# Batch 0's loads, its scores and the written order in a memory-attention and spatial-gate kernel

## The chip, the cores and the metric

One core of one Trainium2 chip runs the program. The metric is the device time of one execution in microseconds (us), lower is better. The engines are named as in the profile: PE (matrix products; PEld is its weight load), DVE (vector engine), ACT (scalar engine), POOL (GpSimd) and SP, which here only issues DMAs.

## The reference

```python
# attention through 32 memory slots; batch 8, 8 heads, 576 positions, head size 64
a   = softmax(phi, over positions)                 # phi: 8 x 8 x 576 x 32
k_m = einsum('bhsm,bhsd->bhmd', a, k)
v_m = einsum('bhsm,bhsd->bhmd', a, v)
attn = softmax(q @ k_m.T / 8)                      # over the 32 slots
x = (attn @ v_m), heads side by side               # 8 x 576 x 512
# gated unit
h = relu(x @ w_in)                                 # 512 -> 1024
u, v = h[..., :512], h[..., 512:]
v_n = (v - mean(v)) / sqrt(var(v) + 1e-6)
v_s = einsum('ts,bsd->btd', w_spatial, v_n) + b_spatial[None, :, None]
out = (u * v_s) @ w_out                            # 512 -> 512
```

w_in and w_out arrive as 64-bit floats, all other inputs as 32-bit floats.

## The kernel before

Eight batches go through the same chain of steps, and up to four batches are under way at a time. Each step is a Python generator with a letter, and each token of a written order advances one generator by one stage. A digit picks a tile (of 128 positions, of 128 channels, or a half of w_in), and each apostrophe means one batch further on. The letters are:

- P (`memory_weights`): phi is loaded, its maximum over positions is taken (DVE, then a transpose on PE `mt`, DVE `cm`, ACT `cmb`, a transpose back on PE `mb`), subtracted on DVE (L334), exponentiated on ACT (L342), and the sum `es` is taken.
- K (`memories`, for batch 0 `first_memories`): k and v are loaded into `kv_sb`, 144 small products with phi make `kvm`, `den` divides, `kmn` and `tk` turn k's part around.
- Q (`queries`, for batch 0 `first_queries`): q is loaded. For batch 0 PE transposes it (`tq`, L530), in later batches DVE does.
- S (`scores`, for batch 0 `first_scores`): q times the 32 memories (`sc`, L559 and L574), softmax on DVE and ACT, and the transposed weights `at`, split in a high part `ah` and a low part `al`.
- M (`products`): the 32 memories of v times one half of w_in, 512 columns wide (`mp`, L727), split into `mh` and `ml`. M1 makes the half for v, M0 the half for u.
- V (`gate`): `pv` (L760), relu, normalisation. U (`units`): `pu` (L844). G (`spatial`): `ps` (L880), fourteen pairs of products for each channel tile. O (`project`): `po` (L917) and the store.

Weights are prepared once, in steps of the same kind: D loads w_in in raw 64-bit words, E and L decode its v half and its u half (ACT, then POOL or ACT, then DVE L198), W loads w_spatial, T0 to T4 transpose it on PE (`wt`, `wr`, L260) and split it, B prepares the bias, X loads and decodes w_out. Z (`warm_up`) is a product of the constant `minus`, 128x128 by 128x512, whose result nothing reads; the order before has none of it.

The order around the change is written by hand: START for the first batches, then PLAN once for each of the batches 2 to 5, then END. Tokens become instructions in this order, and every engine works through its own instructions strictly in it. So an instruction that waits holds up whatever the order has behind it on the same engine. All loads and stores are issued by SP, which waits where a buffer is not yet free. The list `ON_VECTOR` names small operations that go to DVE in place of ACT or POOL. PSUM has eight banks, and every tile that PE writes, one of Z too, takes one of them in turn.

In batch 0 before, q is loaded as 1 KB runs (512 positions as four rows for each partition, then the last 64 positions), and SP issues in the order phi, q, k, rest of q, then weights, with v behind the first weights (L356). Scores of batch 0 are 64 products over 64 rows with 128 weight columns and 32 moving columns (L559), and 16 with 64 weight columns (L574).

## Time and profile before

| what | value |
|---|---|
| time, median of 3 runs | 421.88 us (417.91 to 422.09) |
| the profiled execution, its own time | 420.08 us |
| its span from first to last instruction | 418.3 us |
| PE busy | 395.1 us, 94% |
| DVE busy | 278.7 us, 67% |
| ACT busy | 223.7 us, 53% |
| POOL busy | 91.6 us, 22% |

The times of single instructions come from the one profiled execution. PE's busy time counts each product until its result has left the engine, while the next has begun, so a PE that is busy all the time need not be at its peak; what a product costs in a row of its kind is read from the chain, by the time of the row over its count. The profile also names the clock that PE was granted, as a share of the full 2.4 GHz.

### The profile page before, as it was taken

What the parts mean: (1) busy time and instruction counts of PE and PEld (TensorE: products, weight loads), DVE (VectorE), ACT (ScalarE), POOL (GpSimd) and SP (SyncE); (2) the same over time, 40 slices, a digit from 0 to 9 for tenths busy, and PEclk for the clock granted to TensorE, in tenths of its full rate; (3) what the DMA queues carried; (4) which work ended last, traced back from release to release, by engine and by line L of the source; (5) the groups of instructions that cost most, each with busy time, mean ns of one, the idle gap of its engine ahead of it and who ended that gap; (6) DMA issues with size and microseconds to landing.
All of it is one profiled execution on the core that took longest, in us unless ns stands there. A gap on an engine that the chain in (4) does not pass through costs nothing.

```text
span 418.3 us, 9443 instructions
## 1 busy us (share of the span) xinstructions
PE 395.1 (94%) x3906; PEld 342.8 (82%) x3906; DVE 278.7 (67%) x542; ACT 223.7 (53%) x457; POOL 91.6 (22%) x182
## 2 busy tenths in 40 slices
PE   0997999899999999999899999999999999999996
PEld 0784788688789897989699898989798888988984
DVE  2548989877987648955789258855787349854140
ACT  1436886336862378435853467435853485277122
POOL 1246475002300224013401034013401112032000
PEclk9998999999999999999999999999999999999999
DMA  8996968695572060927085712927400710000203
GB/s 254 328 382 219 199 97 279 121 226 159 84 198 55 25 215 18 258 95 130 2 211 131 132 53 56 228 92 132 53 2 0 133 51 2 0 2 26 76 0 125
DMA packets 86830, 50.69 MB, mean 121 GB/s; under 512 B 66754, under 2 KB 71874, under 8 KB 86788
## 3 DMA queue, kind: packets, MB, share of 16 engines
q1 hardware_dynamic: 86788, 50.10, 48.3%
q8 instruction: 30, 0.49, 0.5%
q14 instruction: 12, 0.10, 0.1%
HBM read 40.65 MB, written 9.44 MB: 120 GB/s over the span
## 4 chain that ended last, share of the span: by engine, by line
PE 80%; DMA 9%; DVE 5%; POOL 3%; issue 2%; ACT 1%; SPq 1%; POOLq 0%; DVEq 0%; ACTq 0%
PE ps L880 22%; PE po L917 22%; PE pu L844 12%; PE pv L760 10%; DMA phi_sb<-in_phi_dram 4%; PE mp L727 3%; PE kvm L434 3%; DMA kv_sb<-in_v_dram 2%; DMA q_all<-in_q_dram 2%; PE sc L559 2%; PE sc L661 1%; DVE phi_sb L334 1%; PE pv L776 1%; PE pv L768 1%; POOL half L289 1%
## 5 line engine op out<-in xcount | busy, mean ns | idle before, releaser
L880 PE MATMUL ps<-wth,vh 128*128 128x288 f32 x256 | 57.5, 304 | 1.1 <-DVE ml L163 0.6
L880 PE MATMUL ps<-wth,vl 128*128 128x288 f32 x256 | 54.7, 295 | 0.9 <-DVE vl L822 0.9
L880 PE MATMUL ps<-wtl,vh 128*128 128x288 f32 x256 | 54.6, 294 | 0.0
L805 DVE BATCH_NORM_STATS2 st<-vr 128x6 f32<-128x512 f32 (+1 forms) x40 | 27.3, 681 | 35.6 <-ACT vr L802 35.3
L917 PE MATMUL po<-woh,gh 128*128 128x512 f32 x128 | 50.4, 394 | 0.0
L917 PE MATMUL po<-woh,gl 128*128 128x512 f32 x128 | 50.0, 390 | 0.0
L917 PE MATMUL po<-wol,gh 128*128 128x512 f32 x128 | 49.9, 390 | 0.0
L923 ACT COPY o<-po 128x512 f32<-128x512 f32 x36 | 21.2, 588 | 53.2 <-PE po L917 35.7
L880 PEld LDWEIGHTS ps<-wth,vh 128*128 128x128 f32 x256 | 41.1, 188 | 5.8 <-issue 1.7
L880 PEld LDWEIGHTS ps<-wth,vl 128*128 128x128 f32 x256 | 40.9, 188 | 1.1 <-DVE vl L822 1.1
L880 PEld LDWEIGHTS ps<-wtl,vh 128*128 128x128 f32 x256 | 41.3, 188 | 0.0
L808 POOL TENSOR_SCALAR few<-few 128x1 f32<-128x1 f32 (+1 forms) x40 | 10.9, 272 | 132.2 <-DVE few L806 118.6
L844 PE MATMUL pu<-ah,mh 128*128 128x288 f32 x128 | 38.7, 302 | 0.0
L822 DVE TENSOR_TENSOR vl<-vr,vh 128x512 fp32r<-128x512 f32 x32 | 23.6, 741 | 21.7 <-ACT vh L820 21.7
L844 PE MATMUL pu<-al,mh 128*128 128x288 f32 x128 | 37.7, 295 | 0.0
L844 PE MATMUL pu<-ah,ml 128*128 128x288 f32 x128 | 37.6, 294 | 0.0
L893 DVE TENSOR_TENSOR g<-u,ps 128x288 f32<-128x288 f32 x64 | 26.5, 443 | 15.4 <-PE ps L880 14.8
L817 ACT ACTIVATE vr<-vr,few 128x512 f32<-128x512 f32 (+1 forms) x40 | 32.0, 816 | 5.2 <-POOL few L812 5.2
L899 ACT CAST gh<-g 128x512 fp32r<-128x512 f32 x32 | 19.7, 619 | 24.5 <-DVE g L893 24.4
L853 ACT ACTIVATE u<-pu 128x288 f32<-128x288 f32 x64 | 25.8, 418 | 5.7 <-PE pu L844 4.1
L917 PEld LDWEIGHTS po<-woh,gl 128*128 128x128 f32 x128 | 24.0, 188 | 5.2 <-DVE gl L901 0.2
L917 PEld LDWEIGHTS po<-woh,gh 128*128 128x128 f32 x128 | 24.0, 188 | 4.7
(174 smaller groups left out, 889.0 us busy)
## 6 DMA issues: line engine op xcount, KB each, us to landing
kv_sb<-in_k_dram SPq DMA_DIRECT2D x8, 1152.0 KB, 8.8
kv_sb<-in_v_dram SPq DMA_DIRECT2D x8, 1152.0 KB, 7.4
out_dram<-o SPq DMA_DIRECT2D x32, 256.0 KB, 2.4
q_sb<-in_q_dram SPq DMA_DIRECT2D x28, 288.0 KB, 8.7
phi_sb<-in_phi_dram SPq DMA_DIRECT2D x7, 576.0 KB, 4.2
raw<-in_moe_w_in_dram SPq DMA_DIRECT2D x4, 512.0 KB, 11.4
raw<-in_moe_w_in_dram SPq DMA_DIRECT2D x2, 1024.0 KB, 10.7
raw_out<-in_moe_w_out_dram SPq DMA_DIRECT2D x4, 512.0 KB, 5.1
```

The costliest lines, as they stand in the source:

```text
L434: nc.tensor.matmul(kvm[r][32 * j : 32 * j + 32], phi_sb[halves[r], j, i, :], kv_sb[halves[r], j, :, i * D : (i + 1) * D], start=(i == 0), ...
L760: nc.tensor.matmul(pv, x[:, r, cs], m[:, r, DM:DFF], start=(n == 0), stop=(n == 5))
L805: nc.vector.bn_stats(st6, vr)
L817: nc.scalar.activation(vr, vr, AF.Identity, bias=sh, scale=rs)
L822: nc.vector.tensor_tensor(vl[:, st, :], vr, vh[:, st, :].bitcast(F32), op=ALU.subtract)
L844: nc.tensor.matmul(pu[hf], m[:, r, cs], a[:, r, at[hf]], start=(r == 0 and n == 0), stop=(r == 1 and n == 2),)
L853: nc.scalar.activation(u[:, dt, at[hf]], pu[hf], AF.Relu)
L880: nc.tensor.matmul(ps[hf], a, w[:, hf * HALF : (hf + 1) * HALF], start=(n == 0), stop=(n == len(ops) - 1),)
L893: nc.vector.tensor_tensor(g[:, at], u[:, dt, at], ps[hf], op=ALU.mult)
L899: nc.scalar.copy(hi, x)
L917: nc.tensor.matmul(po, a, w, start=(n == 0), stop=(n == 11))
L923: nc.scalar.copy(o, po)
```

## The change

Six things are changed together.

- q of batch 0 is loaded in the layout of k and v, one run of nine positions (2,304 bytes) for each partition and pair of heads, and SP's order becomes phi, k, q, v.
- A helper `hold` lets POOL copy one landed element of a given load into the first words of a buffer that another load will fill. That load can then only be issued when the given load has landed and POOL has come to the copy. `HOLD` names the pairs: the two v-half loads of w_in wait for q and for v, the two u-half loads for the first and the third piece of the v half, w_spatial for the fourth.
- Scores of batch 0 become 40 products: two of a partition's nine positions are stacked on 128 rows, the memories `kd` stand on a diagonal of two blocks with zeros beside it (POOL clears it), with 64 weight columns and 64 moving columns (32 for the ninth position). Transposes, softmax and `at` follow the new layout, in three pieces of 16, 16 and 4 groups.
- The sum `es` of batch 0 is taken by four halving steps on DVE in place of one reduction. `kmn1` and `kd1` are added to `ON_VECTOR`.
- START is one order for all eight batches, in which `>` moves the base one batch on. PLAN and END are gone, and with them the loop.
- The order has 56 Z steps. 51 of them stand ahead of the products of M1, of these 10 ahead of `mt`, 3 between `mt` and `mb`, 12 between `mb` and the first `kvm` of batch 0, 4 between there and the first scores.

On PE the new order has one of the five T steps (T0) ahead of the products of M1, where the order before has four. On SP it has, behind v: E00, E01, E10, E11 (the v half of w_in in four pieces), the first quarter of w_out, L0 (first piece of the u half), w_spatial in two loads, L1, the bias. On POOL it has, in this order: hold for q, the clearing of `kd`, hold for v, decode of E00, hold for E00, decode of E10, hold for E11, decode of E01, hold for E10, decode of L0.

```diff
-    P*2 Q P K P*2 Q P Q P Q P*2 Q P Q*2 P*2 K P Q D1 K*3 Q E0*2 K W Q K W K*2 Q K E0 Q S*2 T1 T3 D1
-    T1 S*2 T4 E0*2 S T4 S T3 T1 S D1 E0 S K1 S T3*2 W E1 S*3 K1 S*2 D1 E1 T3 K1 D0 T1 E1 S T3 D0 T1
...
-PLAN = """
-    M0 V1 V4 V0 U0 V3 V1 K' V0 U0 V1 U1 P'' U3 U2 Q' U2 M1 V0 Q' P'' V1 V2 V0 U2*2 V3 U0 P'' S'
...
-END = """
-    V0 V1 U1 V1 U2 Q' V0 U1 V0 V2 U3 V4*2 V1 U0 V0 V4 K' V3 U0 V1 Q' U3 V2 U0 U2 V3 U0 M0' V4*3
...
+    P Z*3 P*3 Z*3 K Z*4 P Z*2 Q P D1 Z P*2 Z*2 P Z*6 P Z K1 P*2 K D1 Z P*2 Z*2 P D1 P K*3 Q Z Q*2 K
+    Z*2 K*2 Q*2 K*2 D1 K Z Q E0 Q K E0 S Q*2 D1 D0 S D1 Z*5 Q Z S*2 K1 E0 S E1 S E1 X0 S K1 E1*2 S
+    Z E1 S*2 Z S K1 Z*3 S E0 W S D0 S Z S Z S Z W Z E0 W K1 E1 D0 L0 E0 Z*3 K1 Z S D0 Z W S Z*2 S
+    T0 L0 T0 S M1 X0 T0 S T4 T0 S T0 T3 Z S L0 X1 T3 T0 S T3 S Z M1*2 P' Z T3 S M1 X0 T1 M1 T3 S*2
...
+    G0'' O1' G0'' G2'' G1'' G0''*2 G3'' G1'' G2''*2 G3'' O4'' O2' G2''*2 O0' G3'' O3'' G3'' O3''
+    O0'' O1'' O1 > G2' O0' O3 > G3 O3 G2 O1 G3 O4 O0 O2 O1 O2 O3 O4 O0 O2 O1 O4 O2
 """
...
...
+
+        source = state["landed", name]
+        nc.gpsimd.tensor_copy(to, source.to_broadcast([1, to.shape[1]]))
+
...
         raws = state["raw", c] = []
         for n in range(2):
             raw = one.tile([P, 2, 2 * 512], I32, tag=(("gh", "gl"), ("vh", "vl"))[c][n], name="raw")
             raws.append(raw)
+            hold(raw[0:1, :, 0], HOLD["LE"[c] + str(n)])
+            yield
             for js in (slice(0, 1), slice(1, 2)) if c else (slice(0, 2),):
                 rows = slice((2 * n + js.start) * P, (2 * n + js.stop) * P)
                 nc.sync.dma_start(
@@ -179,6 +210,7 @@
                     .bitcast(I32)
                     .rearrange("(j p) f -> p j f", p=P),
                 )
+                state["landed", f"{'LE'[c]}{n}{js.start}"] = raw[0:1, js.start, 0:1]
...
@@ -230,6 +262,8 @@
         b_sb = two.tile([P, S], F32, tag="g", name="b_sb")
         state["spatial"] = w_sb, w_rem, b_sb
         nc.gpsimd.memset(b_sb[SR:P], 0.0)
+        hold(w_sb[0:1, 0, 0:1].bitcast(I32), HOLD["W"])
+        yield
...
@@ -342,12 +376,6 @@
             nc.scalar.activation(phi_sb[:, js], phi_sb[:, js], AF.Exp)
             yield
         es = state["es", b] = one.tile([P, NJ, MEM], F32, tag="mx", name="es")
-        if b == 0:
-            nc.vector.tensor_reduce(
-                es, phi_sb.rearrange("p j i m -> p j m i"), axis=AX.X, op=ALU.add
-            )
-            yield
-            return
         yield from over_rows(engine(f"es{b}"), es, ALU.add)
...
     def first_memories(n):
@@ -356,7 +384,12 @@
         nc.sync.dma_start(
             kv_sb[:, :, n, :], x[0].rearrange("(j r) (p i) d -> (r p) j (i d)", r=2, i=NX)
         )
-        yield
+        state["landed", "kv"[n]] = kv_sb[0:1, 0, n, 0:1].bitcast(I32)
+        yield
+        if n == 0:
+            kd = state["kd"] = one.tile([P, 2, NJ, 2, MEM], F32, tag="t1", name="kd")
+            nc.gpsimd.memset(kd, 0.0)
+            yield
...
@@ -386,12 +419,11 @@
         if n == 0:
             kmn = one.tile([P, 2, 2, D], F32, name="kmn")
             for r in range(2):
-                nc.scalar.activation(
-                    kmn[:, r],
-                    kvm[r][:, None, :].to_broadcast([P, 2, D]),
-                    AF.Copy,
-                    scale=den[:, r : r + 1],
-                )
+                x = kvm[r][:, None, :].to_broadcast([P, 2, D])
+                if f"kmn{r}" in ON_VECTOR:
+                    nc.vector.tensor_scalar(kmn[:, r], x, den[:, r : r + 1], None, op0=ALU.mult)
+                else:
+                    nc.scalar.activation(kmn[:, r], x, AF.Copy, scale=den[:, r : r + 1])
                 yield
...
-            kT = state["kT", 0] = one.tile([P, 2, P], F32, name="kT")
-            nc.scalar.copy(kT.rearrange("p r s -> p (r s)"), tk)
-            yield
+            kd = state["kd"]
+            for c in range(2):
+                half = slice(64 * c, 64 * c + 64)
+                to = kd[half, :, :, c, :]
+                x = tk[half].rearrange("p (r j m) -> p r j m", r=2, j=NJ)
+                if f"kd{c}" in ON_VECTOR:
+                    nc.vector.tensor_copy(to, x)
+                else:
+                    nc.scalar.copy(to, x)
+                yield
             return
...
     def first_queries():
-        q_sb = one.tile([P, NX * 4 * D], F32, tag="q_sb", name="q_all")
-        many = q_sb[:, 0 : 4 * H * D].rearrange("p (h i d) -> p h i d", h=H, i=4)
-        last = q_sb[:, 4 * H * D :]
+        q_sb = one.tile([P, NJ, NX * D], F32, tag="q_sb", name="q_all")
         nc.sync.dma_start(
-            many.rearrange("p h i d -> p h (i d)"),
-            q[0, :, 0:SM].rearrange("h (p i) d -> p h (i d)", i=4),
+            q_sb, q[0].rearrange("(j r) (p i) d -> (r p) j (i d)", r=2, i=NX)
         )
-        yield
-        for c in range(2):
-            nc.sync.dma_start(
-                last[64 * c : 64 * c + 64].rearrange("p (h d) -> p h d", d=D),
-                q[0, 4 * c : 4 * c + 4, SM:S].rearrange("h p d -> p h d"),
-            )
-        yield
-        qT = state["qT", 0] = one.tile([P, H * HALF], F32, tag="qT", name="qT")
+        state["landed", "q"] = q_sb[0:1, 0, 0:1].bitcast(I32)
+        yield
+        qT = state["qT", 0] = one.tile([P, 5, NJ * P], F32, tag="qT", name="qT")
...
+            wide = min(2 * D, NX * D - 2 * D * n)
+            for j in range(NJ):
                 nc.tensor.matmul(
-                    tq[:, j * P : (j + 1) * P],
-                    cols,
+                    tq[0:wide, j * P : (j + 1) * P],
+                    q_sb[:, j, 2 * D * n : 2 * D * n + wide],
                     ident,
...
     def first_scores():
-        kT, qT = state.pop(("kT", 0)), state.pop(("qT", 0))
...
-        sc = [bank(f"sc_0_{c}") for c in range(2)]
-        for n in range(2):
-            for h in range(H):
-                for c in range(2):
-                    rows = slice(64 * c, 64 * c + 64)
-                    j, r = h // 2, h % 2
-                    to = (n * 8 + r * 4 + j) * MEM
+        sc = [bank(f"sc_0_{c}") for c in range(3)]
+        for n in range(5):
+            rows = slice(0, P if n < 4 else D)
+            to = sc[n // 2][:, (n % 2) * 256 : (n % 2) * 256 + (256 if n < 4 else P)]
+            to = to.rearrange("p (i j m) -> p i j m", j=NJ, m=MEM)
+            for j in range(NJ):
+                for r in range(2):
+                    half = slice(64 * r, 64 * r + 64)
                     nc.tensor.matmul(
-                        sc[c][:, to : to + MEM],
-                        qT[rows, (n * H + h) * P : (n * H + h + 1) * P],
-                        kT[rows, r, 32 * j : 32 * j + 32],
+                        to[half, :, j],
+                        qT[rows, n, j * P + 64 * r : j * P + 64 * r + 64],
+                        kd[rows, r, j, 0 : 2 if n < 4 else 1],
                         start=True,
                         stop=True,
                     )
-        yield
-        sc += [bank(f"sc_0_{2 + r}") for r in range(2)]
-        for j in range(2):
-            for hh in range(2):
-                for r in range(2):
-                    rows = slice(64 * r, 64 * r + 64)
-                    at = 4 * 512 + j * P + 64 * hh
-                    m = 32 * (2 * hh + j)
-                    nc.tensor.matmul(
-                        sc[2 + r][64 * hh : 64 * hh + 64, j * MEM : (j + 1) * MEM],
-                        qT[rows, at : at + 64],
-                        kT[rows, r, m : m + 32],
-                        start=True,
-                        stop=True,
-                    )
-        yield
+            if n % 2 or n == 4:
+                yield
...
-        for c, cut in enumerate([slice(0, 16), slice(16, 32), slice(32, 34), slice(34, 36)]):
+        for c, cut in enumerate([slice(0, 16), slice(16, 32), slice(32, 36)]):
             x = sc[c][:, 0 : (cut.stop - cut.start) * MEM].rearrange("p (g m) -> p g m", m=MEM)
             nc.vector.tensor_reduce(rmx[:, cut], x, axis=AX.X, op=ALU.max)
             yield
             nc.vector.tensor_tensor(sm[:, cut], x, spread(rmx, cut), op=ALU.subtract)
             yield
-            if c != 2:
-                cut = slice(32, 36) if c == 3 else cut
+            if c != 1:
+                cut = slice(16, 36) if c else cut
                 nc.scalar.activation(sm[:, cut], sm[:, cut], AF.Exp, scale=SCALE)
                 yield
...
         for c in range(3):
             to = bank(f"at_{c}")
-            if c < 2:
...
+            many = 4 if c < 2 else 1
+            for n in range(many):
+                g = 16 * c + 4 * n
+                nc.tensor.matmul(
+                    to[:, n * P : (n + 1) * P],
+                    sm[:, g : g + 4].rearrange("p j m -> p (j m)"),
+                    ident,
+                    is_transpose=True,
+                    start=(n == 0),
+                    stop=(n == many - 1),
+                )
+            yield
+            at = to[:, 0 : many * P].rearrange("q (i r p) -> q i r p", i=many, r=2)
+            x = at.rearrange("q i r p -> q r p i")
+            hv, lv = (
+                y.rearrange("q r (p i) -> q r p i", i=NX)[:, :, :, 4 * c : 4 * c + many]
+                for y in (ah, al)
+            )
...
     def tokens(plan):
-        for kind, n, ahead, times in re.findall(r"([A-Z])(\d?)('*)(?:\*(\d+))?", plan):
+        base = 0
+        for kind, n, ahead, times in re.findall(r"([A-Z>])(\d?)('*)(?:\*(\d+))?", plan):
+            if kind == ">":
+                base += 1
+                continue
             for _ in range(int(times or 1)):
-                yield kind, int(n or 0), len(ahead)
-
-    steps = list(tokens(PLAN))
-    upto, count = {}, {}
-    for at in sorted(range(len(steps)), key=lambda at: -steps[at][2]):
-        key = steps[at][:2]
-        upto[at] = count[key] = count.get(key, 0) + 1
+                yield kind, int(n or 0), 0 if kind in WEIGHTS else base + len(ahead)
     E = mybir.EngineType
     with tc.manual_schedule(engines={E.PE, E.DVE, E.Activation, E.Pool, E.SP}):
-        for kind, n, ahead in tokens(START):
-            step(kind, n, ahead)
-        for b in range(2, B - 2 if END else B):
-            for at, (kind, n, ahead) in enumerate(steps):
-                key = kind, n, b + ahead
-                while b + ahead < B and done.get(key, 0) < upto[at]:
-                    step(*key)
-        for kind, n, ahead in tokens(END):
-            step(kind, n, B - 2 + ahead)
+        for kind, n, b in tokens(START):
+            step(kind, n, b)
```

## Rows read from the trace of the kernel before

**Rows 1.** Stretches of the span (--windows); busy us of PE, PEld, DVE, ACT, POOL, clock, DMA.

```profile
14.40:26.40 12.00, 11.93 (x222) 10.89 (x222) 3.41 (x5) 2.06 (x6) 6.12 (x6) 1.00 1.04 365
26.40:38.04 11.64, 9.20 (x187) 6.70 (x186) 11.22 (x24) 6.18 (x15) 7.84 (x3) 0.94 0.67 243
...
38.04:109.60 71.56, 68.00 (x737) 56.13 (x740) 59.96 (x116) 49.04 (x101) 23.51 (x37) 0.99 0.79 179
109.60:414.00 304.40, 302.14 (x2762) 266.29 (x2761) 199.24 (x393) 161.44 (x327) 52.69 (x126) 1.00 0.37 86
```

**Rows 2.** Timeline of the first 50 us: start, duration, engine, line, what, [idle before].

```profile
6.93 0.30 ACT L327 COPY cmb<-cm 128x128 f32<-128x128 f32 x1 [4.52 <-DVE cm L324]
...
10.45 1.12 PE L530 MATMUL tq<-ident,q_all 128*128 128x128 f32 x4 [3.88 <-DMA q_all<-in_q_dram]
11.35 0.42 PE L330 MATMUL mb<-ident,cmb 128*128 128x128 f32 x1
12.60 1.35 ACT L342 ACTIVATE phi_sb<-phi_sb 128x576 f32<-128x576 f32 x2 [0.41 <-DVE phi_sb L334]
14.43 2.32 PE L366 MATMUL kvm<-kv_sb,phi_sb 64*32 64x64 f32 x144 [0.95 <-ACT qT L543]
19.38 7.04 PE L559 MATMUL sc<-kT,qT 64*128 64x32 f32 x64
26.35 0.65 PE L574 MATMUL sc<-kT,qT 64*64 64x32 f32 x16
26.45 0.69 DVE L588 TENSOR_REDUCE rmx<-sc 128x16 f32<-128x512 f32 x1 [6.90 <-PE sc L559]
26.93 1.11 PE L260 MATMUL wt<-ident,w_sb 128*128 128x128 f32 x4
33.44 0.66 PE L260 MATMUL wt<-ident,w_sb 128*128 128x128 f32 x4
38.04 1.96 PE L727 MATMUL mp<-win_sb,vT 64*32 64x512 f32 x16
46.66 1.09 PE L727 MATMUL mp<-win_sb,vT 64*32 64x512 f32 x16
```

**Rows 3.** Stretches of 5 us (--windows), columns as in rows 1.

```profile
0.00:5.00 5.00, 0.00 (x0) 0.00 (x0) 1.17 (x2) 1.69 (x3) 1.42 (x11) 1.00 0.57 159
5.00:10.00 5.00, 0.45 (x1) 0.18 (x1) 1.27 (x2) 0.30 (x1) 0.00 (x0) 1.00 1.02 340
...
20.00:25.00 5.00, 5.00 (x52) 5.00 (x50) 0.00 (x0) 0.00 (x0) 3.92 (x4) 1.00 1.03 392
```

**Rows 4.** Page, part 6, loads: count, KB each, median us from issue to landing.

```profile
phi_sb<-in_phi_dram SPq DMA_DIRECT2D x2, 288.0 KB, 3.2
```

**Rows 5.** Groups by form (--lines) of PE from 38.04 to 109.60: count, busy, mean ns.

```profile
L844 PE MATMUL pu<-ah,mh 128*128 128x288 f32 x32 | 9.9, 310 | 0.0
L880 PE MATMUL ps<-wth,vh 128*128 128x288 f32 x32 | 7.5, 316 | 0.0
L760 PE MATMUL pv<-mh,ah 128*128 128x512 f32 x16 | 6.6, 414 | 0.6 <-DVE ml L163 0.6
L917 PE MATMUL po<-woh,gh 128*128 128x512 f32 x16 | 6.3, 395 | 0.0
L727 PE MATMUL mp<-win_sb,vT 64*32 64x512 f32 x64 | 5.0, 709 | 0.0
L434 PE MATMUL kvm<-kv_sb,phi_sb 64*32 64x128 f32 x288 | 5.0, 272 | 1.8 <-issue 0.9 <-DMA kv_sb<-in_v_dram 0.7
```

**Rows 6.** The chain that ended last, in order of time: start, us, what.

```profile
66.71 9.71 DMA kv_sb<-in_v_dram
...
166.00 12.55 PE ps L880 x94
...
184.15 2.72 PE po L917 x12
...
192.11 2.39 PE pu L844 x18
```

More of the change, by code (lines that the diff above doesn't have):

```diff
@@ L68 @@
     """
-    es0 es2 es3 ml000 ml001 ml010 ml011 ml100 ml101 ml111 al0 al1 al2 X0.wol X2.wol tq1 tq3 bn0 bn1 bn2 bn3 bn4 wtl00 wtl01 wtl10 wtl11 wtl20 wtl21 wtl30 wtl31 wtl40 wtl41
+    es0 es2 es3 ml000 ml001 ml010 ml011 ml100 ml101 ml111 al0 al1 al2 X0.wol X2.wol tq1 tq3 bn0 bn1 bn2 bn3 bn4 wtl00 wtl01 wtl10 wtl11 wtl20 wtl21 wtl30 wtl31 wtl40 wtl41 kmn1 kd1
     """.split()
@@ L73 @@
 ON_SCALAR = set("E11.lo".split())
+HOLD = {"E0": "q", "E1": "v", "L0": "E00", "L1": "E10", "W": "E11"}
 @with_exitstack
@@ L166, in low, with hold @@
         yield
+    def hold(to, name):
+        source = state["landed", name]
+        nc.gpsimd.tensor_copy(to, source.to_broadcast([1, to.shape[1]]))
     def load_win(b, c):
@@ L599, in first_scores @@
         state["a", 0] = ah, al, ar
-        for c, cut in enumerate((slice(0, 16), slice(16, 36))):
+        for cut in (slice(0, 16), slice(16, 36)):
             nc.vector.tensor_reduce(rsum[:, cut], sm[:, cut], axis=AX.X, op=ALU.add)
@@ L644, in first_scores @@
+            x = at.rearrange("q i r p -> q r p i")
[3 more added lines that the diff above has]
+            )
             nc.scalar.copy(hv, x)
             yield
-            yield from low(f"al{c}", lv, x, hv, places)
+            yield from low(f"al{c}", lv, x, hv, (hv.rearrange("q r p i -> q i r p"), at))
         for n, x in enumerate((ah, al)):
```

143 lines of the change are left out of this document (65 added, 78 removed).

## The prediction

> **What bounds the kernel now.** I read the page's busy shares first: PE at 94% says that only stretches in which it is not fed can give anything. So the table of stretches comes next, to see where they lie. From 109.60 us on PE is busy 302.14 of 304.40 us [rows 1], and the chain that ended last is there almost all PE products, 12.55 us in one piece [rows 6]. A new order has little to win there. Between 38.04 and 109.60 PE is busy 68.00 of 71.56 us. Everything up to 38.04 is preparation: the first products of M1, on which all the large work of batch 0 waits, begin there [rows 2]. So I split the span into 38.04 until M1, 71.56 until 109.60, and the 308.70 that are left of 418.3.
>
> The timeline of the first 50 us shows what sets the 38.04. The copy `cmb` is done at 7.23, but the transpose `mb` that needs it runs at 11.35, since PE stands in q's transposes, which wait 3.88 us for q. Then the scores take 7.04 and 0.65 us, 110 ns for each product with 128 weight columns and 41 ns with 64. Then DVE is the bound: busy 11.22 of 11.64 us from 26.40 to 38.04 [rows 1, 2].
>
> The same timeline shows the clock. The column names the full clock for the first 33 us, yet four transposes take 1.11 us at 26.93 and 0.66 at 33.44, and M1's products 1.96 us at 38.04 against 1.09 for as many at 46.66 [rows 2]. So PE runs at the lower level (1.2 GHz) until about 33 us, and again at 38.
>
> **The change part by part.**
>
> *Loads.* By their shapes phi has 0.59 MB and k, q and v 1.18 MB each. The first 5 us move 0.80 MB (159 GB/s), later stretches 340 to 392 GB/s [rows 3]. In the new order k is in at 7.5 to 7.9, q at 10.5 to 11.3, v at 13.5 to 14.8.
>
> *The phi chain.* `mb` no longer stands behind q. With `cmb` at 7.23 and three idle products in front of it (0.45 each at the lower clock, twice the 0.227 that 2.72 us for twelve products of this shape make [rows 6]) it ends near 8.3 in place of 11.77. From its end to the end of the exponentials it was 2.18 us [rows 2], so 10.5. The twelve idle products behind `mb` take 2.7 us at the full clock, so `kvm` starts at 10.9 in place of 14.43.
>
> *From `kvm` to the scores* it was 4.95 us [rows 2], with six of q's transposes. Now sixteen stand there and four idle products. At the full clock this adds 16 x 0.165 - 6 x 0.28 + 0.9 = 1.9 us (at the lower one 3.7). I take 1.8, as the other steps gain a little from the clock: the scores start at 17.6.
>
> *Scores.* Forty products with 64 weight columns: the nearest row is 0.65 us for sixteen such at the lower clock [rows 2], so 1.6 us for all, against 7.69. The first sixteen, which DVE waits for, take between 0.3 (twice as fast) and 1.8 (110 ns each). I take 0.65, the row of the same width. DVE's first maximum moves from 26.45 to 18.3.
>
> *From there to M1* it was 11.6 us, and DVE was full. The new order gives DVE the same softmax and the same decoding steps ahead of M1, so I leave 11.6: M1 at 29.9. The weights have to be there: 9.1 MB are asked for up to w_spatial, which is in between 26.3 (at 392 GB/s) and 29.5 (at 340). The middle, 27.9, and T0's five transposes (0.83) make 28.7, just hidden. I allow 28.5 to 31.5 for M1.
>
> *At nothing* I put the four steps for `es` (they end while PE is in `kvm`, 2.3 us), the clearing of `kd` (POOL has 4 us for it after q has landed), `kmn1` and `kd1` on DVE (beside their twins on ACT).
>
> *The holds* add waits on POOL and on SP. Behind SP's first one, for q, stand all weight loads and then batch 1's phi, k, v and q. Behind POOL's stand the decodings that M1 needs, and L0 in turn waits for a decoding. I put them at nothing as long as other bytes are moving: E00 is asked for at 11.5 while v moves until 14.8; E10 at 15 while 1.05 MB of E00 and E01 take 3 us; L0 near 19.5 while 1.6 MB of E10, E11 and w_out last until 22; w_spatial at 22.5 while L0 lasts until 24.7; L1 at 26.4 while w_spatial lasts until 28. Without that cover each shows the time of a load from issue to landing, 3.2 us [rows 4].
>
> *Work moved behind M1.* Three T steps that ran before it now run behind it, 3 x 0.83, and five idle products, 5 x 0.227: 3.6 us more.
>
> *The stretch up to 109.60.* Its PE work from counts and prices: 104 products of `pv` and `po` (16 in each of six forms, and eight for the last tile) at 0.227 make 23.6; 112 of `ps` (32 in each of three forms and 16) at 0.1335 make 15.0; 96 of `pu` at 0.133 make 12.8; 64 of `mp` at 0.068 make 4.4; 288 of `kvm` at 0.016 make 4.6; the small ones some 3 [rows 2, 5, 6]. That is 63.4 of 71.56, so 8.2 are lost, though only 3.56 show as idle. By rows 0.87 of it is M1 at the lower clock, and 1.8 the idle time in front of `kvm` [rows 2, 5], for batch 2's v, 9.71 us from issue to landing [rows 6]. The new order has 20.6 us of products between the `kvm` of batch 1 and of batch 2, by these prices, where the old one has 16.5, so both should go. Of the other 5.5, for which no row names a cause, I take one in five as gone: 4.4 stay. Bounds are 1 and 8.2.
>
> *From 109.60 on* the 2.26 us of idle time are the most that an order can win, and it can lose as much. I take 0.7 won.
>
> **The sum.** 29.9 + (63.4 + 3.6 + 4.4) + 308.0 = 409.3 us of span. Around it the profiled execution had 420.08 - 418.3 = 1.8, so 411.1 against its 420.08. That execution lies inside the three runs (417.91 to 422.09), 1.8 below their median; I forecast 411 without moving it. With M1 at 28.5 or 31.5, a loss of 2 or 8.2 and the later part 2 better or 1 worse the same sum gives 405 and 418.
>
> **The rivals.**
>
> *The loss of 8.2 stays.* DVE is busy 59.96 of those 71.56 us [rows 1], nearly as much work as PE's; in a shorter stretch the two may wait for each other as often as before. Then 29.9 + 67.0 + 8.2 + 308.7 = 413.8, with what lies around it 415.6. For it speaks that no row names a cause of 5.5 of the 8.2.
>
> *The clock does not hold.* Between 14.40 and 26.40 PE was busy 11.93 of 12.00 us with small products and transposes, and the transposes after it still ran at the lower level [rows 1, 2]. Idle products stand between such work, four from `kvm` to the scores. If the lower level stays, the twelve cost 2.7 more, the transposes 1.9, M1 0.9: 411.1 + 5.5 = 416.6. [...]
>
> *The holds serialise the weight loads.* This one ends slower. If the decodings on POOL come late, each hold fires into an empty DMA queue, and five times 3.2 us [rows 4] come on M1's path: 411.1 + 16 = 427. It decides from 9 us of gaps on; below that the change still wins. Against it speak the bytes in flight counted above, for it that w_spatial and L1 have only some 2 us of cover. The Trainium skill (DMA: Bandwidth & Descriptors, Rules for kernel authors) asks to issue a DMA early and to wait late, the opposite of a hold, and puts the fixed part of one DMA at about 2.0 us (Anatomy of one DMA); by that the five would cost an estimated 10 us, and no run here shows it yet.
>
> *The late order fits worse.* If each of the last six batches waits 1.5 us more in some strict queue, 9 us go and the time is 420. Against it: PE is 99% busy there already, and most steps have a batch's time of slack.
>
> **How the numbers follow.** What a measurement can tell from no change is about 1%, 4.2 us. Forecast 0.60, the loss stays 0.16, the clock 0.08, the late order 0.09, the holds 0.07. The range 404.5 to 419 takes the forecast's own bounds and the first two rivals, and leaves the last two out. Faster by over 1% (below 417.7) is nearly all of the forecast, most of the first rival and half of the second: 0.74. Slower by over 1% is the holds and a little of the late order: 0.08. Within 1%: 0.18.
>
> **What would show it.** `mb` before q's first transpose; `kvm` near 11; the three score pieces at some 41 ns or less for each product; the first maximum near 18; M1's products near 30 at 1.09 us or so; transposes at 0.66 from early on; DMA busy without a gap until about 30. Wrong would be the forecast if M1 began on time and PE then idled more than 8 us until batch 2's scores, or if idle products delayed `kvm` past 13.

## The result and the profile after

The changed kernel takes 421.42 us (median of 20 runs, 417.14 to 425.40), the one before 419.86 on the same chip (20 runs, 416.30 to 425.35). The ratio is 1.0058, 95% interval 1.0033 to 1.0083: no change by the bound of 1%, if anything slower. (Ratios leave disturbed runs out and medians do not, so the two differ by some tenths of a per cent.) The forecast was 411, its range 404.5 to 419. The profiled execution of the changed kernel has a span of 420.1 us; the prediction's sum was 409.3.

The table of stretches of the changed kernel, cut at the same times as [rows 1] and with the same columns:

```profile
14.40:26.40 12.00, 11.31 (x260) 9.20 (x259) 9.77 (x20) 7.05 (x14) 7.06 (x9) 1.00 0.95 336
26.40:38.04 11.64, 8.09 (x51) 4.79 (x50) 6.48 (x9) 5.11 (x13) 8.46 (x6) 0.85 1.04 366
38.04:109.60 71.56, 68.49 (x868) 57.56 (x869) 61.72 (x122) 48.40 (x100) 26.10 (x43) 1.00 0.76 164
109.60:414.00 304.40, 299.69 (x2611) 263.16 (x2594) 194.67 (x385) 156.12 (x324) 52.17 (x120) 0.99 0.37 84
```

Two things differ. From 26.40 to 38.04 DVE, the bound before, is busy 6.48 of 11.64 us in place of 11.22; PE is not fed either, and its clock fell to 0.85 on average. From 109.60 on, where the prediction expected 0.7 us of idle time to go, PE is busy 2.45 us less than before.

The timeline of the start, to hold against [rows 2] (start, duration, engine, line, what, [idle time before, and what ended it]):

```profile
8.25 0.27 PE L364 MATMUL mb<-ident,cmb 128*128 128x128 f32 x1
9.35 1.35 ACT L376 ACTIVATE phi_sb<-phi_sb 128x576 f32<-128x576 f32 x2 [1.38 <-DVE phi_sb L368]
11.21 1.66 PE L399 MATMUL kvm<-kv_sb,phi_sb 64*32 64x64 f32 x144
13.05 0.64 PE L557 MATMUL tq<-ident,q_all 128*128 128x128 f32 x4
16.45 1.15 PE L586 MATMUL sc<-kd,qT 128*64 128x64 f32 x32 [0.30 <-DVE kd L440]
17.65 0.69 DVE L601 TENSOR_REDUCE rmx<-sc 128x16 f32<-128x512 f32 x1 [0.53 <-PE sc L586]
18.09 1.15 PE L586 MATMUL sc<-kd,qT 128*64 128x64 f32 x32
20.76 0.66 PE L586 MATMUL sc<-kd,qT 64*64 64x32 f32 x16
28.49 0.68 DVE L187 TENSOR_TENSOR al<-at,ah 128x512 fp32r<-128x512 f32 x1
31.54 0.69 PE L294 MATMUL wt<-ident,w_sb 128*128 128x128 f32 x4 [3.46 <-DMA w_sb<-in_moe_w_spatial_dram]
32.60 1.96 PE L724 MATMUL mp<-win_sb,vT 64*32 64x512 f32 x16
...
106.86 1.20 PE L658 MATMUL sc<-qT,kT 64*32 64x288 f32 x32
```

Read it from the top: everything up to the first maximum `rmx` came within 0.3 us of the forecast or before it. Then, at the bottom, PE stands 3.46 us in front of T0's transposes until w_spatial has landed, M1 is behind them in PE's order, and after that idle time M1's sixteen rows take 1.96 us, the lower clock. M1 starts at 32.60, forecast 29.9.

The timeline at two later places of the changed kernel, DVE and PE:

```profile
60.26 0.69 DVE L323 TENSOR_TENSOR half<-phi_sb 128x512 f32<-128x512 f32 x1 [2.12 <-DMA phi_sb<-in_phi_dram]
61.33 0.68 DVE L819 TENSOR_TENSOR vl<-vr,vh 128x512 fp32r<-128x512 f32 x1
62.07 0.54 PE L877 MATMUL ps<-wth,vl 128*128 128x288 f32 x2 [1.33 <-DVE vl L819]
65.55 0.53 PE L877 MATMUL ps<-wth,vl 128*128 128x288 f32 x2 [1.49 <-DVE vl L819]
...
276.50 0.78 DVE L538 STREAM_TRANSPOSE qT<-q_sb 128x576 f32<-128x576 f32 x1 [4.34 <-issue]
277.20 0.65 DVE L898 TENSOR_TENSOR gl<-g,gh 128x512 fp32r<-128x512 f32 x1
281.21 0.79 PE L914 MATMUL po<-woh,gl 128*128 128x512 f32 x1 [2.12 <-DVE gl L898]
282.23 0.63 PE L914 MATMUL po<-wol,gh 128*128 128x512 f32 x1
284.69 0.40 PE L914 MATMUL po<-wol,gh 128*128 128x512 f32 x1
```

It is the same figure twice: DVE stands in front of a step whose load has not landed (batch 2's phi, landed at 60.17; batch 6's q, landed at 276.07, where the row says only "issue"), the gate's subtractions `vl` and `gl` are queued behind it, and PE, which needs them, idles. At 281 the clock falls as well: products of 0.40 us take 0.63.

Three marks of the timelines give the stretches that the prediction added up: the first product of M1, PE's first product of batch 2's scores (106.86 us here, 109.6 before), and the end of the span.

| kernel (one profiled execution each) | M1 at | M1 to scores of batch 2 | from there to the end | span |
|---|---|---|---|---|
| before | 38.0 | 71.6 | 308.7 | 418.3 |
| prediction | 29.9 | 71.4 | 308.0 | 409.3 |
| after | 32.6 | 74.3 | 313.2 | 420.1 |

So 2.7 us are missing in front of M1, 2.9 behind it and 5.2 in the later batches: all 10.8 by which the sum was off. My theory, before the runs below, was two causes. The holds, or T0's place ahead of M1, make w_spatial's arrival the bound of the start, with an echo in batch 2's phi. And the new order of the later batches fits worse. The rivals were that the 56 idle products (12.7 us of PE work) cost what they gain, and that one or two misplaced waits, not the order, are the later loss.

### The profile page after: what moved, and what is told of

It reads as the page before. It is cut to its first block, busy times and chain, and to the rows that moved or that the text cites. A ratio compares the mean times of both kernels' runs of the same rounds, so it can differ in the third digit from the quotient of the medians.

```text
span 420.1 us, 9561 instructions
## 1 busy us (share of the span) xinstructions
PE 401.9 (96%) x3959; PEld 345.9 (82%) x3959; DVE 279.0 (66%) x545; ACT 221.6 (53%) x455; POOL 95.8 (23%) x188
## 4 chain that ended last, share of the span: by engine, by line
PE 81%; DMA 8%; DVE 5%; issue 2%; POOL 1%; ACT 1%; SPq 1%; POOLq 0%; ACTq 0%; DVEq 0%
PE ps L877 27%; PE po L914 23%; PE pv L757 10%; PE pu L841 10%; PE mp L724 3%; DMA kv_sb<-in_v_dram 3%; PE kvm L473 3%; DMA w_sb<-in_moe_w_spatial_dram 2%; PE sc L658 2%; DMA raw<-in_moe_w_in_dram 1%; DMA phi_sb<-in_phi_dram 1%; PE pv L765 1%; PE pv L773 1%; PE wt L294 1%; DVE sm L688 1%
## 5 line engine op out<-in xcount | busy, mean ns | idle before, releaser
L914 PE MATMUL po<-woh,gl 128*128 128x512 f32 x128 | 51.0, 398 | 2.1 <-DVE gl L898 2.1
L914 PE MATMUL po<-woh,gh 128*128 128x512 f32 x128 | 51.3, 401 | 0.2 <-DVE g L890 0.2
L708 POOL CAST ar<-ah 128x128 fp32r<-128x128 f32 x7 | 4.4, 624 | 125.2 <-ACT ah L701 125.2
L805 POOL TENSOR_SCALAR few<-few 128x1 f32<-128x1 f32 (+1 forms) x40 | 9.9, 248 | 99.5 <-DVE few L803 86.6
L914 PEld LDWEIGHTS po<-woh,gl 128*128 128x128 f32 x128 | 24.4, 191 | 7.9 <-DVE gl L898 2.5
L799 ACT ACTIVATE vr<-pv 128x512 f32<-128x512 f32 x32 | 18.9, 598 | 21.7 <-PE pv L757 19.6
```

The costliest lines, as they stand in the source:

```text
L799: nc.scalar.activation(vr, pv, AF.Relu)
L914: nc.tensor.matmul(po, a, w, start=(n == 0), stop=(n == 11))
```

## The experiments

Each verdict is a ratio to the kernel before, measured in turn on the same chip; each mark comes from one profiled execution. The kernels of the runs have more lines of written order than the changed kernel, so the same operation stands some 30 lines further down in their rows (M1's `mp` at L752 to L755 in place of L724), and in early_old 56 lines below its place in the kernel before.

### The order of the later batches

late_old and early_old exchange the order from the scores of batch 2 on:

```diff
 # late_old: START of the changed kernel up to PE's first product of S'' ...
-the changed kernel's tokens from there on
+START, PLAN and END of before: the steps that are still to do
 # early_old: the kernel before, the other way round
```

> The changed kernel's steps up to the scores of batch 2 (PE's first product for them), then the remaining steps in the order of the kernel before. If the gain of the start is given back by the new order of the later batches, the stretch from the scores of batch 2 to the end goes from 313.2 us back to about 308.7, and the time is 421.4 - 4.5 = 417 us, about 0.993 of before. If the later order is innocent, and what is late there comes from the start itself (stores, buffers and decodings that it moved), the stretch stays near 313 and the time is 421.

> The complement: the kernel before up to the scores of batch 2, then the remaining steps in the order of the changed kernel. If the new later order is what gives the gain back, this is before plus 4.5: about 424.4 us, ratio 1.011. If the later order is innocent, it is 420, ratio 1.000.

late_old: 0.9971 (0.9935 to 1.0007). Its stretch from batch 2's scores to the end is 308.4 us, where the changed kernel has 313.2. early_old: 1.0186 (1.0128 to 1.0244), that stretch 316.5. Both lie on the side of the later order's guilt, and late_old has the forecast size: 4.8 us. Two pairs of kernels from the sections below, which also differ in the later order alone, agree: combo 0.9869 beside no_holds 0.9954, and late_m1 0.9940 beside m1_first 1.0037. But early_old lost more than expected, and its timeline shows why it can't be used for the size: 4.16 us lie at the seam itself, in the middle of batch 2's scores, which is neither order's doing:

```profile
111.04 1.49 PE L717 MATMUL sc<-qT,kT 64*32 64x288 f32 x16 [4.16 <-ACT u L909]
```

Where the later order loses can be read from the marks of the later batches, each PE's first product of a batch's scores (us):

| kernel | later order | 2 to 3 | 3 to 4 | 4 to 5 | 5 to 6 | 6 to 7 | 7 to the end |
|---|---|---|---|---|---|---|---|
| before | old | 48.8 | 44.5 | 48.5 | 45.4 | 48.0 | 73.6 |
| late_old | old | 48.4 | 44.9 | 47.3 | 46.0 | 47.9 | 73.8 |
| combo | old | 48.5 | 45.0 | 47.3 | 45.8 | 47.9 | 73.8 |
| after | new | 48.8 | 46.1 | 47.5 | 48.8 | 47.2 | 74.9 |
| no_holds | new | 49.3 | 45.5 | 47.5 | 47.0 | 47.2 | 74.9 |

The last column is the steady part: 74.9 to 75.0 us in all ten profiled kernels with the changed start and the new later order, 73.6 to 73.8 in the seven with the old. From 5 to 6 the new order varies most, from 45.5 us (q6_later) to 49.2 (no_qv_holds).

### Two single waits

DVE's order by tile, shortened:

```diff
 # q6_later: the four DVE transposes of batch 6's q (Q in START) each go behind later steps
-Q gl Q vr bn Q gl bn bn Q vl phisub bn grl
+gl vr bn gl bn bn Q vl Q phisub bn Q grl Q
 # phi2_later: the maximum over phi of batch 2 goes behind vl, t1 and the products with u
-half half vl mx Q mx t1 vl Q cm g g
+vl Q t1 vl Q g g half half mx mx cm
```

> The changed kernel with one move: the four DVE transposes of batch 6's q come some 20 to 30 steps later in the order, behind steps whose inputs have long been there. If this one wait (DVE idle 4.34 us at 272 us, PE idle 2.12 us at 281 and its clock down for 3.4 us behind it) is most of what the later part lost, the loss between the scores of batch 5 and of batch 6 falls from 4.8 to about 1.4 us and the time to 418 us, 0.992 of the changed kernel. If the later order fits worse in many small places, this gives 1 us or less: 420.5 to 421.5.

> The changed kernel with batch 2's maximum over rows of phi moved behind the gate's last two subtractions of batch 0 and the halves of t1 and G0, and the three steps after it as well. If DVE's 2.12 us wait for phi of batch 2 at 58 us is what holds PE up at 60.4 and 63.8 us (1.49 and 1.66 us), those go and the time falls by 2 to 3 us, to 418.5 to 419.5. If PE would wait there in any case (for the gate's values through other engines), or waits later for the scores of batch 1, it stays at 421.

q6_later: 1.0060 (1.0025 to 1.0095), against 1.0058 for the changed kernel: nothing. The wait did go: batch 5's scores to batch 6's take 45.5 us in place of 48.8. But batch 6's to batch 7's take 49.4 in place of 47.2. phi2_later: 1.0113 (1.0058 to 1.0168), nothing won either, perhaps some lost. Its PE waits at 60 and 64 us are gone; two new ones, of 1.44 and 1.45 us, stand at 67 and 70 us, in front of the transpose and the step that need that maximum:

```profile
67.01 0.30 PE L384 MATMUL mt<-ident,mx 128*128 128x128 f32 x1 [1.44 <-DVE mx L358]
70.14 1.45 PE L753 MATMUL mp<-win_sb,vT 64*32 64x512 f32 x16 [1.45 <-DVE phi_sb L397]
```

So the waits were real and moving them was worth nothing. In phi2_later it was the moved maximum itself that came late: phi had landed at 58.4 us, and DVE began on it at 64.75, behind the steps put in front of it. The theory that one or two misplaced steps are the loss fell here, as far as these two waits go.

### The holds

```diff
 def hold(to, name):
+    return                                   # no_holds
+    if name in ("q", "v"): return            # no_qv_holds
+    if name in ("E00", "E10", "E11"): return # no_weight_holds
     source = state["landed", name]
 # no_w_hold: only the call ahead of w_spatial goes
-    hold(w_sb[0:1, 0, 0:1].bitcast(I32), HOLD["W"])
```

> The changed kernel with its five holds left out (the small copies on POOL that make a weight load wait until another has landed), the loads in the same order. If the holds keep the queues short without leaving them empty, as the prediction put them, k, q and v land 1 to 4 us later (k after 9.4, v after 15.4), the scores start after 18 us, and w_spatial lands at 29 to 31, no more than 2 us earlier. If they serialise the loads, w_spatial lands 3 us or more earlier than 31.4 and M1 starts before 30; the time falls with it by 1 to 3 us, to 418 to 420.

> The changed kernel without the one hold ahead of w_spatial; the other four stay. If that hold alone made w_spatial late (it stood on POOL until 23.09 us, behind ACT's decoding), w_spatial lands near 28.5, M1 starts near 30 and the time is that without any holds, 0.995 of before. If each hold takes its share, since a load that is asked for late finds its queue short, w_spatial lands between 29.5 and 31 and M1 starts at 31 to 32: 1.000 to 1.004.

> The changed kernel without the two holds that wait for batch 0's q and v (ahead of E00/E01 and of E10/E11); the three that wait for a piece of the weights stay. If the late start of the first weight loads is what leaves the queues short from 14 to 20 us, E10 is landed before 18 to 19.5, w_spatial at 28.5 to 29.5, M1 starts at 30 to 31 and the time is near that without holds, 0.995 to 0.999. If the later three decide (the next load is asked for only when POOL comes to it), w_spatial stays at 31 and the ratio at 1.004 to 1.007.

> The complement: the holds on q and v stay, those on E00, E10 and E11 (ahead of L0, L1 and w_spatial) go. If the later three decide, w_spatial lands at 28.5 to 29.5 and the ratio is 0.995 to 0.999. If the first two do, w_spatial lands at 30.5 to 32.5 as in the run without the hold ahead of w_spatial, and the ratio is 1.004 to 1.007. If each group leaves its own hole, both runs end between.

| kernel | ratio (95%) | E11 landed | w_spatial landed | M1 at | M1 to batch 2's scores | to the end | span |
|---|---|---|---|---|---|---|---|
| after | 1.0058 (1.0033 to 1.0083) | 21.8 | 31.4 | 32.6 | 74.3 | 313.2 | 420.1 |
| no_holds | 0.9954 (0.9913 to 0.9995) | 20.7 | 28.5 | 29.9 | 71.1 | 311.5 | 412.5 |
| no_w_hold | 1.0073 (1.0039 to 1.0107) | 24.4 | 32.7 | 33.7 | 74.4 | 311.8 | 419.9 |
| no_qv_holds | 0.9969 (0.9941 to 0.9998) | 20.6 | 29.1 | 30.0 | 70.5 | 313.4 | 413.9 |
| no_weight_holds | 1.0037 (0.9993 to 1.0082) | 22.4 | 30.9 | 32.0 | 70.7 | 312.0 | 414.7 |

Without any hold the time falls by about 1% of 420, 4.4 us (late_old and combo, which differ in the holds alone, are as far apart: 0.9971 and 0.9869), and M1 starts at 29.9, the forecast to the tenth. My expectation had it wrong for the prediction's side: k, q and v did not land later (9.46, 12.46 and 15.42 us; with the holds 9.43, 12.42 and 15.36), so the holds protected nothing. The Trainium skill (DMA: Bandwidth & Descriptors, Queues, rings and completion order) says that each DMA engine takes the descriptors of one ring in order; the trace agrees, as these three landings show. In each of the 18 profiled executions the loads landed in the order in which SP issued them, so here a later load needed no hold to stay behind.

What the holds cost is seen in the rate. The same three stretches of the changed kernel (last column GB/s, the one before it the DMA engines' busy share):

```profile
14.00:20.00 6.00, 5.70 (x89) 4.80 (x88) 4.10 (x7) 3.57 (x8) 3.28 (x4) 1.00 0.99 353
20.00:26.00 6.00, 5.61 (x175) 4.47 (x174) 5.27 (x13) 3.48 (x8) 3.38 (x6) 1.00 0.93 319
26.00:32.00 6.00, 2.54 (x16) 1.80 (x14) 3.17 (x4) 1.80 (x3) 3.63 (x2) 1.00 1.02 348
```

and of no_holds:

```profile
14.00:20.00 6.00, 5.34 (x85) 4.44 (x84) 3.77 (x7) 3.10 (x8) 2.14 (x2) 1.00 1.03 413
20.00:26.00 6.00, 4.71 (x171) 3.75 (x170) 5.28 (x13) 3.64 (x9) 4.61 (x4) 1.00 1.04 380
26.00:32.00 6.00, 5.95 (x47) 4.09 (x45) 4.14 (x7) 3.44 (x8) 4.21 (x5) 1.00 1.02 329
```

From 14 to 26 us 353 and 319 GB/s stand against 413 and 380: 6 us times 60 and 61 GB/s are 0.73 MB less by 26 us, some 2 us at these rates. It is not one execution's chance: from 14 to 20 us the eight profiled kernels with all five holds moved 272 to 353 GB/s at a busy share of 0.82 to 0.99, the five without any 408 to 415 at 1.03; w_spatial landed at 30.4 to 32.9 in the eight, at 28.5 to 29.2 in four of the five and at 30.8 in the fifth (combo_m1_ahead, whose v landed late, at 17.8). The page's list of loads shows what a full queue looks like, first after, then no_holds (count, KB each, us from issue to landing):

```profile
raw<-in_moe_w_in_dram SPq DMA_DIRECT2D x4, 512.0 KB, 3.9
w_sb<-in_moe_w_spatial_dram SPq DMA_DIRECT2D x1, 1152.0 KB, 8.1
```

```profile
raw<-in_moe_w_in_dram SPq DMA_DIRECT2D x4, 512.0 KB, 13.3
w_sb<-in_moe_w_spatial_dram SPq DMA_DIRECT2D x1, 1152.0 KB, 16.0
```

The later figures are not slower loads, but loads asked for long before: w_spatial is issued at 12.47 us in place of 23.30 and lands 2.9 us earlier. In the changed kernel its hold ran at 23.09 us on POOL, behind ACT's decoding of E11:

```profile
23.09 0.18 POOL L195 COPY w_sb<-raw 1x1 int32<-1x1 int32 x1 [1.69 <-ACT raw L224]
```

Which hold is it? I took it for that one, and was wrong: without it alone nothing changes, and in that execution the weights asked for ahead of it came later (E11 at 24.4). The holds on q and v carry most of it: without these two the ratio is 0.9969 and w_spatial lands at 29.1; without the other three 1.0037 and 30.9. The intervals of these two overlap a little, so the share of the other three stays open. The row of no_weight_holds in the table flatters it: its profiled execution took 416.5 us, the median of its twelve is 419.5.

Behind M1 the echo goes too. In no_holds phi of batch 2 is issued at 50.80 and landed at 54.80 us (after: 54.56 and 60.17), DVE does not wait for it, and neither of PE's two waits for `vl` is there. But this part does not hang on the holds themselves. It goes with the clock at M1, as m1_first (below) shows, which has all five holds, w_spatial at 31.4 us as in the changed kernel and M1 at 32.53, but at the full clock. From there to batch 2's scores it takes 71.6 us in place of 74.3, PE never waits for `vl`, and DVE waits only 0.66 us for phi:

```profile
58.45 0.72 DVE L352 TENSOR_TENSOR half<-phi_sb 128x512 f32<-128x512 f32 x1 [0.66 <-DMA phi_sb<-in_phi_dram]
```

The others fall in with it. Where M1 ran at the full clock (no_holds, no_qv_holds, no_weight_holds, m1_first, combo, combo_m1) this stretch took 70.5 to 71.6 us and phi landed 3.9 to 4.1 us after its issue; where the clock was down there (after, late_old, late_m1, q6_later, no_w_hold) it took 73.1 to 75.8 and phi 5.1 to 5.6. Why phi takes longer then is not shown. So the holds cost in two ways: w_spatial is late, and in these five PE's wait for it was followed by the lower clock. The mean granted clock of all executions fits this: its median is 0.992 for the changed kernel, 0.996 for no_qv_holds, 1.000 for no_holds and 0.999 for combo. A missing 0.008 of 420 us is 3.4 us, an estimate of the most that the clock can have taken.

### M1's place behind T0

```diff
 # m1_first, late_m1 (late_old with it), combo_m1 (combo with it)
-T0 L0 T0 S M1
+L0 T0 S M1 T0
 # m1_ahead, combo_m1_ahead
-T0 L0 T0 S M1
+L0 S M1 T0 T0
```

> The changed kernel with one step moved: the first products of M1 stand ahead of T0's transposes on PE. If PE's wait for w_spatial (3.46 us, to 31.54) is what makes M1 late, and the idle time what takes its clock, M1 starts at about 29.4 us (the first al of the softmax ends at 29.17) and takes 1.1 us at the full clock in place of 1.96. If M1's start sets what follows, the scores of batch 2 come 3 us earlier, at 104, and the time is 3 us less, 418. If the gate of batch 0 waits for w_spatial and the second half of the weights in any case, only M1 moves, the first pv stays at 38 to 39 us and the time at 421.

> Both together: M1's first products ahead of T0, and from the scores of batch 2 on the order of the kernel before. If the two are separate, the later stretch is 304 to 305 us (from the scores of batch 2 to the last product) and M1 starts at 29.4: the span is that of the later old order alone, 415.1, less 0 to 3 us, 412 to 415, and the ratio to before 0.988 to 0.997. If the gain at M1 is eaten up before the scores of batch 2, it is 415 and 0.997.

> The same with M1's first products ahead of T0. Without holds w_spatial lands at 28.5 and the first al of the softmax ends near 29, so M1 has no wait left that this could spare: the start of M1 moves by less than 1 us and the time is that of the kernel without the move within 1 us. If w_spatial still is what decides, it is 1 to 2 us less.

The first edit did not do what I meant. A token is a step's turn, not its content: T0's next token still stood ahead of M1 and did the transposes, and only ACT's rounding after them moved. So these three are near repeats: 1.0037 (0.9989 to 1.0085), 0.9940 (0.9906 to 0.9973) and 0.9869 (0.9829 to 0.9909), beside 1.0058, 0.9971 and 0.9869. They show how far two runs of nearly the same order lie apart, 0.003. One thing they show of the start: in m1_first w_spatial landed at 31.4 us, as in the changed kernel, but the softmax was later, and PE worked on idle products and small steps until then. Its clock was down from 26.4 to 30.0 us (0.53 on average), over idle products for the most part, and M1 had the full clock again:

```profile
31.57 0.63 PE L323 MATMUL wt<-ident,w_sb 128*128 128x128 f32 x4
32.53 1.09 PE L753 MATMUL mp<-win_sb,vT 64*32 64x512 f32 x16
```

> The changed kernel with M1's first products really ahead of T0's transposes on PE: both of T0's first two steps now stand behind them (with one moved, as before, T0's next step did the transposes in the old place). M1's inputs are there at 27.8 us (its half of the weights) and 27.1 (v's memories), so it starts near 28.1 at the full clock. If T0's wait for w_spatial only changes its place, PE idles 2 to 3 us behind M1 in place of in front of it, the first pv comes 1 to 2 us earlier than 38.6 and the time is 420. If M1's start is what the batch waits for, the first pv comes at 34 to 35 and the time is 417.

> No holds, the later order of the kernel before, and M1 really ahead of T0. Without holds w_spatial lands at 28.5 to 29.1, when PE comes to T0 in any case, so there is at most 0.7 us of wait to spare: M1 starts at 28.5 to 29.5, the scores of batch 2 at 100 to 101, the span is 408 to 409.5 and the ratio 0.985 to 0.988. If M1's place matters by itself, the ratio is 0.982.

m1_ahead: 1.0054 (1.0017 to 1.0092). M1 does start at 28.4, and nothing comes of it:

```profile
28.39 1.69 PE L753 MATMUL mp<-win_sb,vT 64*32 64x512 f32 x16
32.35 0.63 PE L323 MATMUL wt<-ident,w_sb 128*128 128x128 f32 x4 [2.27 <-DMA w_sb<-in_moe_w_spatial_dram]
35.32 2.07 PE L962 MATMUL idle<-minus 128*128 128x512 f32 x3
40.14 0.79 PE L786 MATMUL pv<-mh,ah 128*128 128x512 f32 x1
```

The wait for w_spatial stands behind M1 now, the clock falls for the idle products and for `pv` behind it, and the first `pv` comes at 40.1 (after: 38.6). combo_m1_ahead: 0.9826 (0.9774 to 0.9879), 412.44 us, where combo (below) has 412.21 and 0.9869. M1's place is worth nothing that these runs can tell; in the changed kernel w_spatial's arrival is the bound.

### The idle products

```diff
 # no_idle: the changed kernel, combo_no_idle: combo (below)
-every Z
```

> The changed kernel without any of its 56 idle products (12.7 us of PE work at 0.227 us each). If they pay, the clock is at its lower level for the first 30 us or more, kvm starts later than 11.2 less 1, q's transposes take 1.1 us for four and the scores start 1 to 3 us later than 16.45; M1, which waits for w_spatial, stays within 1 us of 32.6, so that the time is 420 to 423. If they cost what they gain, the first products behind them come earlier and the loss after M1 is the same: the time is 1 to 3 us less, 418 to 420.

> The first of these without the 56 idle products. If they pay now, since PE has no long wait left in front of M1, M1's products run at the lower clock (1.96 us for sixteen in place of 1.09) and start 1 to 4 us later than 29.9; the time is 2 to 4 us more. If they only cost what they gain, as in the changed kernel itself, it is the same within 1 us.

no_idle: 1.0060 (1.0017 to 1.0102), where the changed kernel has 1.0058: over the whole kernel they cost what they gain. The marks say where: in the profiled executions they bring batch 2's scores forward by 2.7 us (106.9 against 109.5), and from there the changed kernel takes 313.2 us, no_idle 309.1. That is the one kernel in which the new later order is nearly as short as the old (307.5 to 309.7); the other nine lie between 311.4 and 313.4. What makes it shorter there is not shown. q's first twelve transposes took 2.80 us without them, 0.93 for four against 0.64, but PE then waited 5.82 us for w_spatial in place of 3.46. combo_no_idle: 0.9976 (0.9949 to 1.0004) against 0.9869 for combo. Once the other waits are gone, the 12.7 us of idle products give back 1.1% more than they cost, 4.5 us. Three stretches of combo:

```profile
24.00:30.00 6.00, 5.23 (x38) 3.82 (x26) 5.18 (x11) 3.39 (x8) 3.70 (x4) 1.00 1.04 325
30.00:38.00 8.00, 7.99 (x55) 5.66 (x56) 7.36 (x13) 7.07 (x16) 6.38 (x4) 1.00 1.05 385
48.00:68.00 20.00, 19.37 (x271) 17.23 (x258) 17.76 (x37) 14.72 (x33) 10.03 (x16) 1.00 0.67 209
```

and of combo_no_idle:

```profile
24.00:30.00 6.00, 2.55 (x54) 1.90 (x31) 4.87 (x11) 3.02 (x7) 3.56 (x3) 0.53 1.05 314
30.00:38.00 8.00, 7.87 (x45) 4.38 (x45) 5.40 (x9) 5.40 (x12) 6.82 (x4) 0.71 1.05 386
48.00:68.00 20.00, 17.19 (x243) 15.20 (x249) 15.79 (x29) 12.49 (x29) 9.43 (x15) 0.91 0.67 183
```

M1 starts only 0.45 us later without them (30.64 against 30.19), but the clock is 0.53 from 24 to 30 us and 0.71 from 30 to 38, so M1 and the products behind it are slow, and by batch 2's scores 5.9 us are lost (106.8 against 100.9).

### The two causes taken away together

```diff
 # combo: late_old and no_holds in one kernel
```

> The changed kernel without its holds, and from the scores of batch 2 on the order of the kernel before. If the two losses are separate, the scores of batch 2 start at 101 us as without the holds alone, the later stretch is 304 to 305 us, the span 409 (near the 409.3 of the prediction's sum) and the ratio to before 0.982 to 0.988. If the earlier start runs into the later order's loads and stores, it is 0.993 to 0.996.

combo: 0.9869 (0.9832 to 0.9907), 412.21 us against 418.11, faster than both kernels. M1 at 30.2, 70.7 to batch 2's scores, 308.3 to the end, span 409.2: the prediction's three terms were 29.9, 71.4, 308.0 and 409.3.

## Why the prediction was wrong

*Where the start is bound: right before the change, wrong after it.* The chain of phi came as worked out: `mb` ended at 8.5 (8.3), the exponentials at 10.7 (10.5), `kvm` started at 11.2 (10.9), the first maximum at 17.65 (18.3). The loads came later than worked out, k, q and v at 9.4, 12.4 and 15.4 us (forecast 7.5 to 7.9, 10.5 to 11.3, 13.5 to 14.8), with and without the holds; `kvm` did not wait for them. Four of q's transposes took 0.64 us in place of 1.12 [rows 2], the full clock, so the rival of a clock that does not hold failed where it was placed; the clock fell later, in front of M1, behind a wait, and the 0.9 us that this rival put there came (1.96 in place of 1.09). The 3.7 us that the sum would add between `kvm` and the scores at the lower clock left the four idle products at the full one; with them it is 4.6. "From there to M1 it was 11.6 us" is right as work for DVE, which was done with the first part of the weights `al` at 29.17. But DVE was no longer the bound.

*"I put them at nothing" is the step that failed first.* The holds cost about 4.4 us. They made w_spatial 2.9 us late, M1 waited for it, and in five profiled executions with such a wait M1 then ran at the lower clock. The argument that other bytes are moving was true and not enough: the rate fell from 413 to 353 GB/s while bytes were moving. My own estimate of w_spatial, 27.9 between 26.3 and 29.5, is met without holds (28.5 in no_holds) and missed with them (31.4). The rival "the holds serialise the weight loads" had the mechanism; its price, five times 3.2 us, was too high, since a held load does not find the queue empty but short. The Trainium skill's rule to issue a DMA early and to wait late (DMA: Bandwidth & Descriptors, Rules for kernel authors) was quoted with it, and by that rule, which spoke against this change, the trace agrees: 0.9954 without the holds, 1.0058 with them. The estimate of 10 us beside it is more than twice what was measured; the section it goes by gives its 2.0 us for DMAs that GpSimd issues, and here SP issues them.

*The stretch behind M1.* 71.4 was right where M1 ran at the full clock and batch 2's phi came in time (71.1 in no_holds, 70.7 in combo). The 74.3 of the changed kernel are M1 at the lower clock and PE's two waits for `vl`: the 0.87 us for M1's clock, which I let go, stayed. Over the 67.0 of work the loss is 4.1 in no_holds and 3.7 in combo, forecast 4.4, and 7.3 in the changed kernel itself, nearer to the rival in which 8.2 stay. That rival's reason, DVE and PE waiting for each other as often as before, is out, since the loss went in no_holds with the same work.

*The later batches are the second failed step.* "0.7 won" and the bound "it can lose as much" (2.26) took PE's idle time as the measure of what an order can do. It lost 4.5 us (313.2 against 308.7), and 3.2 without the holds (311.5 in no_holds, 308.3 in combo); both are differences of single executions, and the ratios give some 0.9% of 420, 3.7 us. That bound holds for gains only: an order can lose any time. The rival "the late order fits worse" was right in kind, at half its price of 9 us. Its place is not one batch: what q6_later won in one it lost in the next, and only the 1.2 us from batch 7's scores to the end are there in every kernel. Why the new order is worse, step for step, stays open.

*Scores: the size of a term.* I put forty products at 1.6 us. They are 80 instructions (32, 32 and 16 in the rows above) and took 2.96: each of these products (true float32, no transpose) is two instructions in the trace, and the counts of [rows 2] are instructions, as is the "64 products" and "16" that the section on the kernel before gives. It lay off the path: the first 32 instructions, sixteen products, took 1.15 us in place of 0.65, and the first maximum still came early.

*Idle products.* Their cost was counted right, 12.7 us. What they are worth was not asked: nothing over the whole changed kernel, 4.5 us in combo.

*The size of what can be told.* One execution of the kernel before had M1 at 38.0, early_old, with the same start, at 35.7. The sum and the table rest on single executions, and some 2 us of a start are within their spread.

## What to carry to other kernels

Don't gate a load on the landing of an earlier one to keep bandwidth for it: in these runs the loads of one queue landed in the order of issue without it, k, q and v no more than 0.1 us later, and the gate cost rate behind them. When a stage is shortened, ask anew which input arrives last there, and read an order's PE idle time as the bound of its gains, never of its losses. A step that pays nothing in one kernel (idle products here) can pay 1% once the wait behind it is gone, so test it again then.

## What was not expected of the hardware

The DMA engines' busy share says little of the rate: in no_holds it was 1.03, 1.04 and 1.02 in three stretches that moved 413, 380 and 329 GB/s, and in the changed kernel 0.99 at 353 GB/s.

A short stop of PE in the midst of a full run was followed by the lower clock: behind the 2.12 us of idle time at 281 us, six products of the 0.40 us kind took 0.63 each, starting 0.43 us apart in place of 0.23. That is 6 x 0.2 = 1.2 us on top of the wait. But not every such stop does it. In no_weight_holds PE waited longer, 2.66 us, and what came behind ran at the full clock:

```profile
31.07 0.63 PE L325 MATMUL wt<-ident,w_sb 128*128 128x128 f32 x4 [2.66 <-DMA w_sb<-in_moe_w_spatial_dram]
32.00 1.09 PE L755 MATMUL mp<-win_sb,vT 64*32 64x512 f32 x16
```
